# Decay attention and two feed-forward layers on one core: in the first group of each layer every pair of feature tiles takes plain products, and the fourth input sum is made later

## The chip, the core and the metric

The kernel runs as one program on one core of a Trainium2 chip. The time is device time in microseconds (us) of that core, from launch to the last output. Five engines work side by side, each through its own list of instructions in the order in which the program put them there: TensorE (PE) multiplies, with weight loads (PEld) that overlap it; VectorE (DVE), ScalarE (ACT) and GpSimd (POOL) work on tiles in on-chip memory; SyncE (SP) issues transfers. An instruction waits on semaphores until its operands are made and its buffer is free, and whatever stands behind it on its engine waits too.

## The reference

```python
def _attn_ref(q, k, v, lam):              # 2 batches, 8 heads, 768 tokens, head width 64
    ...
    for b in range(nb):                   # blocks of 64 tokens, a state carried from one to the next
        intra = einsum(einsum(qb, kb) * Dmask, vb)
        inter = einsum(qb * lam_pow, kv_state)
        out[:, :, sl] = intra + inter
        kv_state = lam_block * kv_state + einsum(kb * rev_pow, vb)

def _moe_ref(x, w_in, w_out):             # x: 1536 x 512, w_in: 512 x 2048, w_out: 2048 x 512
    h = x @ w_in
    g = h * np.tanh(softplus(h))
    return g @ w_out

def _moe2_ref(x, w_in, w_out):            # the same shapes
    h = x @ w_in
    g = h * sigmoid(h)
    return g @ w_out
```

The attention's output, 1536 tokens of 512 channels, goes through two feed-forward layers without a residual. All data are float32.

## The kernel before, in words

**Precision.** A float32 operand is cut into a high part, rounded by a cast to the matmul's format, and a low part, the difference. A product of two operands is three matmuls: high by high, low by high, high by low. ACT makes the high part (a cast), POOL or DVE the low part (a subtraction). Weights arrive as raw words and DVE first makes a value of them in five instructions (`split_op`, L122 to L138, tile `dec`); in the second layer ACT does the first of the five (L94). Then ACT casts (`wh`) and POOL subtracts (`wl`, `run_parts`, L173).

**Tiles.** Tokens stand in three blocks of 512 (block 0, 1, 2). The 2048 hidden features of a layer are 16 tiles of 128; four tiles are a group, so there are eight groups, g = 0 to 3 in the first layer and 4 to 7 in the second. Two neighbouring tiles are a pair, two pairs to a group. Tile n has an input weight (n,0) and an output weight (n,1).

**Products.** An input product (`emit_h`, L407: 12 matmuls of 128x512 into a bank `ph`) gives one tile of hidden features for one block. `activate` then puts three things behind it: the activation on ACT (`wa`), the cast `gh` on ACT, the low part `gl` on POOL. An output product (`emit_o`, L425: 12 matmuls into four banks `po`) adds that tile to the block's output. After the last tile of a group, `evac` (L457) adds the four banks to `acc` on DVE (in a layer's first group ACT copies them). At the end of the first layer ACT casts `acc` to the next layer's input `xh` and POOL makes `xl`, four of each per block (L474 to L481); the list `rest` holds POOL's part and is drained one entry per item by `run_rest`.

**Block products.** For a pair of feature tiles and token blocks 0 and 1, `Block` (L528) replaces the four input products by seven half-size ones, `m1` to `m7`, of six matmuls each. They need sums of parts of the input (tiles `sh`, `sl`, four sums, made once per layer by `make_sums` in the first and in `evac` in the second) and sums of the pair's weights (`sum_pair`, L145: four subtractions on DVE, tiles `th`, `tl`). Between the seven, ACT copies two intermediate results (`b`, L568; `m5`, L573) and DVE adds two (`c` and `e`, L557). The fourth input sum takes the place of a part of block 1's input (`sums[3]` is `x1[0][:, 0:2]`, L513), so it may be written only after the last plain product of block 1 in that group. Pairs in `plain` (L82) go without block products: pairs 2 and 8, the first pair of groups 1 and 4.

**Order.** The program is written as a list of items per group (L678 to L728). Each item runs its functions and then a few instructions from other lists: `run_parts` (casts and low parts of weights that are ready), `run_rest`, `run_sums` (one entry of the list of input sums) and `run_split(k)` (k instructions of the list of weight splits). Output products of block 2 of a group run as `fills` among the next group's items. Groups 1 and 4 (`first`) begin with four plain input products of pair A, with fills between them, then a block product of pair B among output products, then the output products of block 1 and the input products of block 2 in turn. The other groups have a block product for each pair.

Of the kernel before, what the change touches and what calls it, by code (L numbers as in the profile page):

```python
# [7 lines left out]
F32 = mybir.dt.float32  # L8
# [9 lines left out]
def decay_attention_mish_silu_kernel(  # L18
# [8 lines left out]
    nc = tc.nc  # L27
    P = 128
# [50 lines left out]
    parts = []  # L79

    pre = []
    plain = (2, NF // 2)  # L82
    silu = []
    uses = {}

# [371 lines left out]
    def evac(mm, g, t):  # L457
# [13 lines left out]

        xh, xl = x_tile(t)

        def part(j):  # L474
            nc.scalar.copy(xh[:, j, :], acc[:, j, :])
            rest.append((
                (t, j),
                lambda: nc.gpsimd.tensor_tensor(  # L478
                    out=xl[:, j, :], in0=acc[:, j, :], in1=xh[:, j, :].bitcast(F32), op=ALU.subtract
                ),  # L480
            ))  # L481

        if t != 1:
            for j in range(4):
                part(j)
            return
        a1, a2 = accs[0, 0], acc

# [2 lines left out]
        add, sub = ALU.add, ALU.subtract  # L491
        drain = lambda: run_rest(len(rest))
        summing.extend([
            [tt(f1, a2[:, 0:2], a2[:, 2:4], add)],
            [cast(0, f1), lambda: part(0), lambda: part(1)],
            [low(0, f1), lambda: part(2), lambda: part(3), tt(f1, f1, a1[:, 0:2], sub)],
            [drain, cast(1, f1), tt(f4, f4, f1, sub)],
            [low(1, f1), tt(f3, a1[:, 0:2], f3, sub)],
            [cast(2, f3)],
            [low(2, f3)],  # L500
# [7 lines left out]
    def make_sums():  # L508

        x0, x1 = x_tile(0), x_tile(1)  # L510
        sh, sl = [late[0].tile([P, 3, 2, T], F32R, tag=t, name=t, bufs=1) for t in ("sh", "sl")]
        sums.extend((sh[:, i], sl[:, i]) for i in range(3))
        sums.append((x1[0][:, 0:2], x1[1][:, 0:2]))  # L513
        q = lambda xt, k: [xt[i][:, 2 * k : 2 * k + 2].bitcast(F32) for i in (0, 1)]
        a11, a12, a21, a22 = q(x0, 0), q(x0, 1), q(x1, 0), q(x1, 1)
        tmp = late[1].tile([P, 4, T], F32, tag="acc", name="tmp")
        f1, f2 = tmp[:, 0:2], tmp[:, 2:4]
        f3 = late[0].tile([P, 2, T], F32, tag="t4", name="s3", bufs=1)
        add, sub = ALU.add, ALU.subtract
        summing.extend([  # L520
            [tt(f1, a21[0], a22[0], add), tt(f1, f1, a21[1], add), tt(f1, f1, a22[1], add), tt(f2, f1, a11[0], sub)],
            [cast(0, f1), tt(f2, f2, a11[1], sub), tt(f3, a11[0], a21[0], sub), tt(f3, f3, a11[1], add), low(0, f1)],
            [cast(1, f2), tt(f1, a12[0], f2, sub), tt(f1, f1, a12[1], add), tt(f3, f3, a21[1], sub), low(1, f2)],
            [cast(2, f3), low(2, f3)],
        ])
        last_sum.append([cast(3, f1), low(3, f1)])

    class Block:  # L528

# [105 lines left out]
    for i, (t, f) in enumerate(steps):  # L635
# [6 lines left out]
            make_sums()  # L642
        if i == len(steps) - 1:
            split_pair(3)
            sum_pair(3)
        for half in halves.get(i, ()):
            split_w(*half)
        if n < N:
# [29 lines left out]
    for g in range(1, 2 * NG):  # L678
# [1 line left out]
        pa = n0 // 2  # L680
        A, B = Block(pa), Block(pa + 1)
        o = lambda t, f, a=False, b=False: lambda: emit_o(t, n0 + f, a, b)

        os = [(0, 0), (0, 1), (0, 2), (0, 3), (1, 1), (1, 0), (1, 3), (1, 2)]
        if g == 1:
            os = os[4:] + os[:4]
        os = [o(t, f, i % 4 == 0, i % 4 == 3) for i, (t, f) in enumerate(os)]
        hs = [lambda n=n0 + f: emit_h(2, n) for f in range(GF)]
        sp = lambda fn, *a: lambda: fn(*a)
        more = pa + 2 < NF  # L690
        nxt = [[lambda p=p: split_pair(p)] if p < NF else [] for p in (pa + 2, pa + 3)]
        if nxt[0]:
            nxt[0].append(lambda: sum_pair(pa + 2))
        fill = [[fn, sp(split_w, n0 + j, 1)] for j, fn in enumerate(fills + [idle] * (4 - len(fills)))]
        first = g in (1, NG)
        if g > 1:
            fill[0].append(lambda: sum_pair(pa + 1))
        fill[3] += nxt[0]
        if first:

            order = ((1, 1), (1, 0), (0, 0), (0, 1)) if g == 1 else ((0, 0), (0, 1), (1, 1), (1, 0))
            ha = [[lambda t=t, n=n0 + f: emit_h(t, n)] for t, f in order]
            ha[1 if g == 1 else 3].append(lambda: summing.append(last_sum.pop()))
            items = [it for i in range(4) for it in (ha[i], fill[i])]
        else:
            items = [[A.m1], [A.m5], fill[0], [A.m2], [A.m6], fill[1], [A.m7], [A.m3], fill[2], [A.m4], fill[3]]
        items += [
            [B.m1], [B.m5], [B.m2], [B.m6], [os[0]], [B.m7], [B.m3], [os[1]], [B.m4], [os[2]], [os[3]],
            [hs[0]], [os[4]], [hs[1], *nxt[1]], [os[5]], [hs[2]], [os[6]], [hs[3]], [os[7]],
        ]  # L710
        for at, item in enumerate(items):
            if g == NG and at == 7:
                silu.append(True)
# [2 lines left out]
            for fn in item:  # L716
                fn()
            run_parts(k)
            run_rest(0 if g == NG and 7 <= at < 14 else 1)
            run_sums(1)  # L720
            small = isinstance(getattr(item[0], "__self__", None), Block)
            k = 1 if small else 0 if item[0] is idle else 3 if item[0] in hs or at < (18 if first else 11) else 2
            if g == NG and at < 8:
                k = (0, 1, 1, 1, 1, 3, 3, 3)[at]
            elif g == NG - 1 and at == len(items) - 1:
                k = 0
            run_split(k)
# [51 lines left out]
```

## Time and profile before

| | |
|---|---|
| median of three runs | 606.63 us (605.3 to 607.45) |
| the profiled execution | 607.67 us, its span 605.9 us |
| PE busy | 575.0 us, 95% of the span, 2870 matmuls |
| DVE / ACT / POOL busy | 418.2 / 239.2 / 325.5 us |
| TensorE's granted clock | 0.979 of full speed on average |
| transfers | 50.55 MB, 83 GB/s over the span |

The page's first part is the busy time of each engine, its second cuts the span into 40 slices of 15 us: a digit is the busy share of a slice in tenths, and the PEclk line is the clock that TensorE was granted. Since PE is busy nearly all the time, what is worth reading is where it isn't: a stretch of PE's timeline where starts lie farther apart than elsewhere, the wait printed in brackets, and what the engine named there was itself waiting for.

### The profile page before, as it was taken

The numbers are of one execution on the slowest core, as the hardware profiler recorded it, in microseconds if no ns is written. First come the engines' busy times: TensorE is split into PE (matmuls) and PEld (weight loads), VectorE is DVE, ScalarE is ACT, GpSimd is POOL, SyncE is SP. The second block draws the span as 40 slices with busy tenths as digits, with TensorE's granted clock in tenths as the row PEclk, the third lists the DMA queues.
The fourth block names the chain that finished last, engine by engine and source line by source line (L and its number), as shares of the span: only waits on it lengthen the run. The fifth ranks groups of instructions, "written<-read, shape, count | busy, mean of one in ns | idle before, by whom it ended". The sixth has DMA issues, their size and how long they took to land. (4 is left out here: it accounts for less than half of the span.)

```text
span 605.9 us, 7515 instructions
## 1 busy us (share of the span) xinstructions
PE 575.0 (95%) x2870; PEld 469.3 (77%) x2870; DVE 418.2 (69%) x520; ACT 239.2 (39%) x439; POOL 325.5 (54%) x237
## 2 busy tenths in 40 slices
PE   7899999997899999999999859999999999999997
PEld 4777778886678888888887647788788878888886
DVE  3898963799858687768797779838834895567102
ACT  2435442436413334324426244446433542353220
POOL 1758783346446365646494548737554646445320
PEclk8999999999989999999999879999999999999999
DMA  7955720012322122312221112222402131200103
GB/s 253 421 179 165 288 70 1 1 35 70 104 67 73 36 69 76 98 36 70 70 70 36 35 35 70 69 70 70 133 6 70 46 102 62 70 1 1 70 0 138
DMA packets 14627, 50.55 MB, mean 83 GB/s; under 512 B 1528, under 2 KB 3072, under 8 KB 13312
## 3 DMA queue, kind: packets, MB, share of 16 engines
q1 hardware_dynamic: 14592, 50.08, 24.3%
q8 instruction: 22, 0.36, 0.2%
q14 instruction: 13, 0.11, 0.1%
HBM read 46.92 MB, written 3.15 MB: 83 GB/s over the span
## 5 line engine op out<-in xcount | busy, mean ns | idle before, releaser
L403 POOL TENSOR_TENSOR gl<-wa,gh 128x512 fp32r<-128x512 f32 x96 | 143.8, 1504 | 130.6 <-ACT gh L402 49.1
L179 POOL TENSOR_TENSOR wl<-dec,wh 128x512 fp32r<-128x512 f32 x64 | 88.4, 1381 | 84.9 <-ACT wh L178 84.8
L465 DVE TENSOR_TENSOR acc<-po,acc 128x512 f32<-128x512 f32 x72 | 46.4, 685 | 73.8 <-PE po L441 73.8
L399 ACT ACTIVATE wa<-ph 128x512 f32<-128x512 f32 x48 | 28.8, 599 | 154.2 <-PE ph L418 138.6
L441 PE MATMUL po<-gh,wh 128*128 128x512 f32 x192 | 76.8, 400 | 1.3 <-ACT wh L178 1.3
L418 PE MATMUL ph<-xl,wh 128*128 128x512 f32 x192 | 73.8, 392 | 4.0 <-POOL xl L478 4.0
L441 PE MATMUL po<-gh,wl 128*128 128x512 f32 x192 | 76.1, 396 | 0.9 <-POOL wl L179 0.9
L138 DVE SCALAR_TENSOR_TENSOR dec<-slot,dec 128x512 uint32<-128x512 uint32 x64 | 74.8, 1168 | 1.9
L418 PE MATMUL ph<-xh,wh 128*128 128x512 f32 x192 | 75.7, 394 | 0.2 <-ACT xh L359 0.2
L441 PE MATMUL po<-wl,gh 128*128 128x512 f32 x192 | 74.8, 390 | 0.9 <-POOL wl L179 0.9
L441 PE MATMUL po<-wh,gl 128*128 128x512 f32 x192 | 74.7, 389 | 0.0
L441 PE MATMUL po<-wh,gh 128*128 128x512 f32 x192 | 74.7, 389 | 0.0
L132 DVE TENSOR_SCALAR dec<-dec 128x512 f32<-128x512 f32 x64 | 47.4, 740 | 34.7 <-ACT dec L94 33.6
L136 DVE SCALAR_TENSOR_TENSOR dec<-slot,dec 128x512 uint32<-128x512 uint32 x64 | 60.6, 947 | 2.1
L402 ACT CAST gh<-wa 128x512 fp32r<-128x512 f32 x96 | 58.4, 623 | 1.1
L178 ACT CAST wh<-dec 128x512 fp32r<-128x512 f32 x64 | 39.6, 619 | 44.7 <-DVE dec L138 44.7
L418 PE MATMUL ph<-xh,wl 128*128 128x512 f32 x192 | 53.5, 393 | 0.0
L441 PE MATMUL po<-gl,wh 128*128 128x512 f32 x192 | 51.9, 392 | 0.0
L134 DVE TENSOR_SCALAR dec<-dec 128x512 uint32<-128x512 uint32 x64 | 49.7, 777 | 2.0
L179 POOL TENSOR_TENSOR tl<-t,th 128x512 fp32r<-128x512 f32 x24 | 33.6, 1408 | 24.6 <-ACT th L178 21.0
L418 PEld LDWEIGHTS ph<-xl,wh 128*128 128x128 f32 x192 | 36.0, 188 | 13.0 <-POOL xl L478 5.7
L441 PEld LDWEIGHTS po<-gh,wh 128*128 128x128 f32 x192 | 36.7, 191 | 10.3 <-ACT wh L178 1.7
(106 smaller groups left out, 962.2 us busy)
## 6 DMA issues: line engine op xcount, KB each, us to landing
slot<-w SPq DMA_DIRECT2D x64, 512.0 KB, 3.7
xslot<-x SPq DMA_DIRECT2D x10, 1024.0 KB, 9.0
out<-acc SPq DMA_DIRECT2D x12, 256.0 KB, 2.1
xslot<-x SPq DMA_DIRECT2D x4, 512.0 KB, 4.4
dmask<-scr SPq DMA_DIRECT2D x2, 256.0 KB, 4.5
lamrow<-scr SPq DMA_DIRECT2D x2, 128.0 KB, 6.7
pw<-lam SPq DMA_DIRECT2D x1, 0.0 KB
scr<-pw SPq DMA_DIRECT2D x1, 8.0 KB
```

Of the source, the lines that this page charges most:

```text
L132: nc.vector.tensor_scalar(out=df, in0=df, scalar1=2.0**-15, scalar2=None, op0=ALU.max)
L134: nc.vector.tensor_scalar(out=d, in0=d, scalar1=3, scalar2=0x3FFFFFF8, op0=shl, op1=band)
L136: nc.vector.scalar_tensor_tensor(out=d, in0=low, scalar=29, in1=d, op0=shr, op1=bor)
L138: nc.vector.scalar_tensor_tensor(out=d, in0=high, scalar=0xC0000000, in1=d, op0=band, op1=bor)
L178: nc.scalar.copy(hi, f)
L179: nc.gpsimd.tensor_tensor(out=lo, in0=f, in1=hi.bitcast(F32), op=ALU.subtract)
L399: nc.scalar.activation(a, ps, AF.Mish if mm == 0 else AF.Silu)
L402: nc.scalar.copy(gh, a)
L403: nc.gpsimd.tensor_tensor(out=gl, in0=a, in1=gh.bitcast(F32), op=ALU.subtract)
L418: nc.tensor.matmul(ph, lhsT=wi[wsel][:, kk * P : (kk + 1) * P], rhs=xt[xsel][:, kk, :], start=(i == 0), stop=(i == 3 * KD - 1),)
L441: nc.tensor.matmul(po[t][j], lhsT=lhsT, rhs=rhs, start=(first and wsel + gsel == 0), stop=(last and gsel == 1))
L465: nc.vector.tensor_tensor(out=acc[:, j, :], in0=po[t][j], in1=acc[:, j, :], op=ALU.add)
```

## The change

Pairs 3 and 9 become plain as well, so groups 1 and 4 have no block products at all, and blocks remain in five groups. Those two groups now run: eight plain input products of blocks 0 and 1 (the first four with the fills between them, the last four in turn with the four output products of block 0), then the input products of block 2 in turn with the output products of block 1. The fourth input sum of the first layer is no longer made with the other three but by `fourth`, after the last plain product of block 1, from the second sum's high and low parts in a tile of its own. In the second layer the casts to `xh` of block 1 stand in `evac` itself, ahead of the sums, and POOL's subtractions are drained at the second entry of the list of sums instead of the fourth. The weight sums of pairs 3 and 9 go; those of pairs 4 and 10 are asked for later in the group.

```diff
-    plain = (2, NF // 2)
+    plain = (2, 3, NF // 2, NF // 2 + 1)
...
-        def part(j):
+        for j in range(4):
             nc.scalar.copy(xh[:, j, :], acc[:, j, :])
             rest.append((
...
         if t != 1:
-            for j in range(4):
-                part(j)
             return
...
         summing.extend([
+            [], [drain],
             [tt(f1, a2[:, 0:2], a2[:, 2:4], add)],
-            [cast(0, f1), lambda: part(0), lambda: part(1)],
-            [low(0, f1), lambda: part(2), lambda: part(3), tt(f1, f1, a1[:, 0:2], sub)],
-            [drain, cast(1, f1), tt(f4, f4, f1, sub)],
+            [cast(0, f1)],
+            [low(0, f1), tt(f1, f1, a1[:, 0:2], sub)],
+            [cast(1, f1), tt(f4, f4, f1, sub)],
...
-            [cast(1, f2), tt(f1, a12[0], f2, sub), tt(f1, f1, a12[1], add), tt(f3, f3, a21[1], sub), low(1, f2)],
+            [cast(1, f2), tt(f3, f3, a21[1], sub), low(1, f2)],
...
-        last_sum.append([cast(3, f1), low(3, f1)])
+        def fourth():
+            f4 = late[0].tile([P, 2, T], F32, tag="t4", name="s4", bufs=1)
+            h2, l2 = (s.bitcast(F32) for s in sums[1])
+            for fn in (tt(f4, a12[0], h2, sub), tt(f4, f4, a12[1], add), tt(f4, f4, l2, sub)):
+                fn()
+            summing.append([cast(3, f4), low(3, f4)])
+        last_sum.append([fourth])
...
-            sum_pair(3)
...
-        if nxt[0]:
+        if nxt[0] and not first:
             nxt[0].append(lambda: sum_pair(pa + 2))
...
         if first:
-            order = ((1, 1), (1, 0), (0, 0), (0, 1)) if g == 1 else ((0, 0), (0, 1), (1, 1), (1, 0))
-            ha = [[lambda t=t, n=n0 + f: emit_h(t, n)] for t, f in order]
-            ha[1 if g == 1 else 3].append(lambda: summing.append(last_sum.pop()))
-            items = [it for i in range(4) for it in (ha[i], fill[i])]
+            hp = [[lambda t=t, n=n0 + f: emit_h(t, n)] for t in range(2) for f in range(GF)]
+            hp[-1].append(lambda: summing.append(last_sum.pop()))
+            items = [it for i in range(4) for it in (hp[i], fill[i])]
+            items += [it for i in range(4) for it in (hp[4 + i], [os[i]])]
+            items.append([hs[0], lambda: sum_pair(pa + 2)])
...
-            run_rest(0 if g == NG and 7 <= at < 14 else 1)
+            run_rest(0 if g == NG and 7 <= at < 12 else 1)
...
-                k = (0, 1, 1, 1, 1, 3, 3, 3)[at]
+                k = (1, 1, 1, 2, 2, 2, 2, 2)[at]
```

Three places in the engines' lists follow, each before and after. Numbers behind names tell buffers apart and differ between the two programs.

ACT early in group 1, before. The high part of the weight (4,1) (`wh1_1284`) stands ahead of an activation, its cast, and the copy `b` of the block product.

```order
L399 ACTIVATE wa_1358<-ph_1343 128x512
L402 CAST gh_1356<-wa_1358 128x512
L178 CAST wh1_1284<-dec_1286 128x512
L399 ACTIVATE wa_1386<-ph_1371 128x512
L402 CAST gh_1384<-wa_1386 128x512
L568 COPY b_1406<-a_1399 128x512
L573 COPY m5_1417<-e_1410 128x512
```

ACT at the same place after (`wh1_1278`, `wh1_1325` and `wh1_1358` are the high parts of (4,1), (5,1) and (6,1)).

```order
L399 ACTIVATE wa_1346<-ph_1331 128x512
L178 CAST wh1_1278<-dec_1280 128x512
L402 CAST gh_1344<-wa_1346 128x512
L178 CAST wh1_1325<-dec_1327 128x512
L399 ACTIVATE wa_1376<-ph_1361 128x512
L402 CAST gh_1374<-wa_1376 128x512
L399 ACTIVATE wa_1407<-ph_1392 128x512
L402 CAST gh_1405<-wa_1407 128x512
L178 CAST wh1_1358<-dec_1360 128x512
```

The copies `b` and `m5` are gone; the casts of weights stand among activations of plain products.

ACT in group 4, before: the casts of block 2's input (`xh_802`) and what stands behind them.

```order
L402 CAST gh_2893<-wa_2895 128x512
L475 CAST xh_802<-acc_1328 128x512 x4
L178 CAST th_2903<-t4_2876 128x512
L94 ACTIVATE dec_2940<-slot3_87 128x512
L94 ACTIVATE dec_2944<-slot1_85 128x512
L568 COPY b_2953<-a_2946 128x512
L573 COPY m5_2964<-e_2957 128x512
L178 CAST wh1_2836<-dec_2838 128x512
```

ACT at the same place after; `wh1_2823` is the high part of (17,1), and `ph_2931` is the first input product of block 1.

```order
L402 CAST gh_2884<-wa_2886 128x512
L475 CAST xh_802<-acc_1319 128x512 x4
L178 CAST wh1_2823<-dec_2825 128x512
L94 ACTIVATE dec_2921<-slot3_87 128x512
L94 ACTIVATE dec_2925<-slot1_85 128x512
L94 ACTIVATE dec_2929<-slot0_84 128x512
L399 ACTIVATE wa_2946<-ph_2931 128x512
L402 CAST gh_2944<-wa_2946 128x512
```

What stood behind the four casts was a copy on which the next matmuls wrote; it is now a weight's cast and an activation.

POOL in group 4, before: the four low parts of block 2's input (`xl_803`).

```order
L179 TENSOR_TENSOR wl1_2837<-dec_2838,wh1_2836 128x512
L403 TENSOR_TENSOR gl_2980<-wa_2981,gh_2979 128x512
L179 TENSOR_TENSOR wl1_2909<-dec_2910,wh1_2908 128x512
L478 TENSOR_TENSOR xl_803<-acc_1328,xh_802 128x512
L403 TENSOR_TENSOR gl_3032<-wa_3033,gh_3031 128x512
L403 TENSOR_TENSOR gl_3036<-wa_3037,gh_3035 128x512
```

POOL at the same place after, from the low part of (17,1) to the last of the four.

```order
L179 TENSOR_TENSOR wl1_2824<-dec_2825,wh1_2823 128x512
L403 TENSOR_TENSOR gl_2945<-wa_2946,gh_2944 128x512
L179 TENSOR_TENSOR wl1_2869<-dec_2870,wh1_2868 128x512
L403 TENSOR_TENSOR gl_2985<-wa_2986,gh_2984 128x512
L179 TENSOR_TENSOR wl1_2920<-dec_2921,wh1_2919 128x512
L478 TENSOR_TENSOR xl_803<-acc_1319,xh_802 128x512
L403 TENSOR_TENSOR gl_3023<-wa_3024,gh_3022 128x512
L478 TENSOR_TENSOR xl_803<-acc_1319,xh_802 128x512
L179 TENSOR_TENSOR wl0_2924<-dec_2925,wh0_2923 128x512
L478 TENSOR_TENSOR xl_803<-acc_1319,xh_802 128x512
L403 TENSOR_TENSOR gl_3063<-wa_3064,gh_3062 128x512
L478 TENSOR_TENSOR xl_803<-acc_1319,xh_802 128x512
```

The first of block 2's low parts follows the low part of (19,1), where it followed that of (18,1), and a `gl` or a weight's low part stands between each two of the four.

## Rows read from the trace of the kernel before

**Rows 1.** The page's parts 1 and 2: busy time by engine, and TensorE's granted clock by slice.
```profile
PE 575.0 (95%) x2870; PEld 469.3 (77%) x2870; DVE 418.2 (69%) x520; ACT 239.2 (39%) x439; POOL 325.5 (54%) x237
...
PEclk8999999999989999999999879999999999999999
```

**Rows 2.** Stretches of the span: from:to, length, busy us (instructions), PEclk, DMA.
```profile
144.08:171.31 27.23, 21.74 (x79) 16.76 (x78) 20.34 (x25) 9.94 (x18) 16.80 (x13) 0.87 0.30 97
171.31:320.92 149.61, 149.61 (x662) 123.87 (x660) 113.20 (x148) 54.13 (x95) 83.82 (x59) 1.00 0.21 66
320.92:382.71 61.79, 49.94 (x199) 39.01 (x198) 50.30 (x48) 27.23 (x45) 38.32 (x25) 0.92 0.15 47
382.71:605.90 223.19, 218.46 (x961) 179.75 (x959) 126.04 (x162) 87.74 (x157) 105.10 (x76) 1.00 0.18 59
```

**Rows 3.** Timeline of PE, first stretch: start, us, line, tiles, count, [idle, releaser].
```profile
146.34 0.61 PE L549 MATMUL e<-sl,th 128*128 128x512 f32 x2
150.30 1.07 PE L549 MATMUL a<-xh,wh 128*128 128x512 f32 x2 [3.35 <-ACT b L568]
...
165.71 0.50 PE L441 MATMUL po<-gh,wh 128*128 128x512 f32 x1 [1.25 <-ACT wh L178]
```

**Rows 4.** Timeline of ACT in the first stretch.
```profile
148.00 0.62 ACT L178 CAST wh<-dec 128x512 fp32r<-128x512 f32 x1 [3.44 <-DVE dec L138]
...
149.67 0.58 ACT L568 COPY b<-a 128x512 f32<-128x512 f32 x1
```

**Rows 5.** Timeline of DVE around the first stretch.
```profile
128.51 1.52 DVE L130 TENSOR_SCALAR dec<-slot 128x512 uint32<-128x512 uint32 x1
130.06 0.43 DVE L132 TENSOR_SCALAR dec<-dec 128x512 f32<-128x512 f32 x1
...
137.17 0.43 DVE L164 TENSOR_TENSOR t<-dec 128x256 f32<-128x256 f32 x1
...
142.26 0.41 DVE L130 TENSOR_SCALAR dec<-slot 128x512 uint32<-128x512 uint32 x1
...
146.31 1.66 DVE L138 SCALAR_TENSOR_TENSOR dec<-slot,dec 128x512 uint32<-128x512 uint32 x1
...
162.37 1.40 DVE L132 TENSOR_SCALAR dec<-dec 128x512 f32<-128x512 f32 x1
```

**Rows 6.** Timeline of PE, second stretch.
```profile
337.69 0.50 PE L418 MATMUL ph<-xl,wh 128*128 128x512 f32 x1 [1.47 <-POOL xl L478]
...
358.69 1.22 PE L549 MATMUL a<-xh,wh 128*128 128x512 f32 x2 [7.03 <-ACT b L568]
```

**Rows 7.** Timeline of ACT in the second stretch.
```profile
354.10 2.41 ACT L475 CAST xh<-acc 128x512 fp32r<-128x512 f32 x4 [4.44 <-DVE acc L465]
...
358.06 0.57 ACT L568 COPY b<-a 128x512 f32<-128x512 f32 x1
```

**Rows 8.** Groups by line and shape: busy us, mean ns, idle before, releaser.
```profile
L403 POOL TENSOR_TENSOR gl<-wa,gh 128x512 fp32r<-128x512 f32 x96 | 143.8, 1504 | 130.6 <-ACT gh L402 49.1 <-PE b L549 41.1 <-issue 30.6
L179 POOL TENSOR_TENSOR wl<-dec,wh 128x512 fp32r<-128x512 f32 x64 | 88.4, 1381 | 84.9 <-ACT wh L178 84.8
...
L478 POOL TENSOR_TENSOR xl<-acc,xh 128x512 fp32r<-128x512 f32 x12 | 20.1, 1689 | 0.0
```

**Rows 9.** Timeline of DVE in the second stretch.
```profile
304.31 1.52 DVE L130 TENSOR_SCALAR dec<-slot 128x512 uint32<-128x512 uint32 x1
...
312.01 1.51 DVE L130 TENSOR_SCALAR dec<-slot 128x512 uint32<-128x512 uint32 x1
...
320.44 2.48 DVE L465 TENSOR_TENSOR acc<-po,acc 128x512 f32<-128x512 f32 x4 [1.63 <-PE po L441]
...
336.43 2.28 DVE L455 TENSOR_TENSOR acc<-acc 128x1024 f32<-128x1024 f32 x1
...
353.38 2.47 DVE L465 TENSOR_TENSOR acc<-po,acc 128x512 f32<-128x512 f32 x4
```

**Rows 10.** Timeline of POOL in the second stretch.
```profile
368.83 1.47 POOL L478 TENSOR_TENSOR xl<-acc,xh 128x512 fp32r<-128x512 f32 x1
```

More of the change, by code (lines that the diff above doesn't have):

```diff
@@ L477, in part @@
                 (t, j),
-                lambda: nc.gpsimd.tensor_tensor(
+                lambda j=j: nc.gpsimd.tensor_tensor(
                     out=xl[:, j, :], in0=acc[:, j, :], in1=xh[:, j, :].bitcast(F32), op=ALU.subtract
@@ L682, in decay_attention_mish_silu_kernel @@
         o = lambda t, f, a=False, b=False: lambda: emit_o(t, n0 + f, a, b)
-        os = [(0, 0), (0, 1), (0, 2), (0, 3), (1, 1), (1, 0), (1, 3), (1, 2)]
-        if g == 1:
-            os = os[4:] + os[:4]
+        first = g in (1, NG)
+        os = [(0, 0), (0, 1), (0, 2), (0, 3)] + [(1, f) for f in (range(4) if first else (1, 0, 3, 2))]
         os = [o(t, f, i % 4 == 0, i % 4 == 3) for i, (t, f) in enumerate(os)]
@@ L691, in decay_attention_mish_silu_kernel @@
         nxt = [[lambda p=p: split_pair(p)] if p < NF else [] for p in (pa + 2, pa + 3)]
-        if nxt[0]:
+        if nxt[0] and not first:
             nxt[0].append(lambda: sum_pair(pa + 2))
         fill = [[fn, sp(split_w, n0 + j, 1)] for j, fn in enumerate(fills + [idle] * (4 - len(fills)))]
-        first = g in (1, NG)
-        if g > 1:
+        if not first:
             fill[0].append(lambda: sum_pair(pa + 1))
@@ L699, in decay_attention_mish_silu_kernel @@
         if first:
-            order = ((1, 1), (1, 0), (0, 0), (0, 1)) if g == 1 else ((0, 0), (0, 1), (1, 1), (1, 0))
-            ha = [[lambda t=t, n=n0 + f: emit_h(t, n)] for t, f in order]
-            ha[1 if g == 1 else 3].append(lambda: summing.append(last_sum.pop()))
-            items = [it for i in range(4) for it in (ha[i], fill[i])]
+            hp = [[lambda t=t, n=n0 + f: emit_h(t, n)] for t in range(2) for f in range(GF)]
[3 more added lines that the diff above has]
+            items.append([hs[0], lambda: sum_pair(pa + 2)])
         else:
             items = [[A.m1], [A.m5], fill[0], [A.m2], [A.m6], fill[1], [A.m7], [A.m3], fill[2], [A.m4], fill[3]]
[L707 to L710, printed above, removed]
+            items += [
+                [B.m1], [B.m5], [B.m2], [B.m6], [os[0]], [B.m7], [B.m3], [os[1]], [B.m4], [os[2]], [os[3]], [hs[0]],
+            ]
+        items += [[os[4]], [hs[1], *nxt[1]], [os[5]], [hs[2]], [os[6]], [hs[3]], [os[7]]]
         for at, item in enumerate(items):
@@ L718, in decay_attention_mish_silu_kernel @@
             run_parts(k)
-            run_rest(0 if g == NG and 7 <= at < 14 else 1)
+            run_rest(0 if g == NG and 7 <= at < 12 else 1)
             run_sums(1)
             small = isinstance(getattr(item[0], "__self__", None), Block)
-            k = 1 if small else 0 if item[0] is idle else 3 if item[0] in hs or at < (18 if first else 11) else 2
+            k = 1 if small else 0 if item[0] is idle else 3 if item[0] in hs or at < (8 if first else 11) else 2
             if g == NG and at < 8:
-                k = (0, 1, 1, 1, 1, 3, 3, 3)[at]
+                k = (1, 1, 1, 2, 2, 2, 2, 2)[at]
             elif g == NG - 1 and at == len(items) - 1:
```

## The prediction

> **What bounds the kernel now.** I read the page's first part, then the granted clock by slice, then a table of stretches, then the timelines of PE, ACT and DVE around the two places where PE loses time. PE is busy 95% of the span [rows 1], so the kernel is bound by the number of matmuls, apart from what PE loses in few places. The clock line shows where: it leaves 9 at the very start, in slices 12 and 23 to 24 [rows 1]. The table of stretches gives the loss. From 171.31 to 320.92 us, 660 weight loads (each belongs to one matmul) take 149.61 us: 0.2267 us a matmul, and PE is never idle. At that step the 78 matmuls from 144.08 to 171.31 would take 17.68 us and take 27.23: 9.55 us lost. The 198 from 320.92 to 382.71 would take 44.89 and take 61.79: 16.90 us lost. The 959 after 382.71 would take 217.4 of 223.19 us, and most of the rest is the end of the program [rows 2]. The first stretch is the middle of group 1, the second the first half of group 4: the two groups that the change rewrites. Together they lose 26.45 us.
>
> **Why PE waits there.** In the first stretch the block product `m2` waits 3.35 us for ACT's copy `b` [rows 3]. That copy did not wait for data: on ACT it stood behind the cast of the weight (4,1), which waited 3.44 us for DVE and began at 148.00 us [rows 4], the moment when DVE's last instruction on that weight ended (146.31 + 1.66) [rows 5]. A late weight stops a product that doesn't need it, since the cast is ahead in ACT's list. Later an output product waits for its own weight's cast, 1.25 us [rows 3]. The matmuls behind such a wait run slowly: two take 1.07 us where two took 0.61 before it [rows 3], and the granted clock of the stretch is 0.87 [rows 2], between the levels 2.4 and 1.2 GHz. In the second stretch an input product of block 1 waits for POOL's `xl`, up to 1.47 us each time, and then `m2` waits 7.03 us for `b` [rows 6], which on ACT stood behind four casts of block 2's input that waited 4.44 us for DVE to add up block 2's output [rows 7].
>
> **The change, part by part.** The sum is made against the profiled execution, 607.67 us (span 605.9), which is 1.04 above the median of the runs shown, 606.63.
>
> *More matmuls.* A plain pair is 2 tiles x 2 blocks x 12 = 48 matmuls, a block product 7 x 6 = 42. Two pairs: 12 more, 12 x 0.2267 = +2.72 us, all on the path, since PE is it.
>
> *Work that goes from other engines.* Eight weight subtractions and four adds (DVE), four casts and four copies (ACT), four low parts (POOL); one 1024-wide instruction more for the fourth sum (DVE). Off PE they are worth nothing by themselves; their place in the lists counts below. SP issues the same loads in the same order.
>
> *First stretch: its 9.55 us go.* Up to 144.08 us both programs run the same count of products. From there the new one runs an input product of block 1, then the output products with (4,1), (5,1), (6,1), (7,1) at 146.80, 152.24, 157.68 and 163.12 us (a product is 12 x 0.2267 = 2.72). What is late next, the weights? DVE began (6,0) at 128.51 and ended (7,0) at 137.17, and (4,1) took from 142.26 to 147.97 [rows 5]: (8.66 + 5.71) / 3 = 4.79 us a weight. From 137.17 to 142.26, 5.09 us, it made the weight sums of pair 3 and the fourth sum's low part [rows 5], which no longer stand there. So (4,1) to (7,1) end at 141.96, 146.75, 151.54, 156.33; a cast (0.62, [rows 4]) and a low part (1.38, [rows 8]) later they are 2.8 to 4.8 us ahead of PE. The fourth sum now stands ahead of the addition of block 0's output, whose banks the product at 168.56 needs: (8,0) ends at 161.1, three 1024-wide instructions at up to 2.28 [rows 9] at 168.0, two short ones follow, and the first addition ends about 170. That costs 0 to 2 us; I take 0, since the 2.28 was beside POOL. The copies `b` that PE waited for don't exist any more; the group's activations have four banks and don't hold PE.
>
> *Second stretch: its 16.90 us go, and a new wait of 6.3 comes.* Block 1's `xl` was the first wait; its casts now follow DVE's additions of 320.44 to 322.92 [rows 9] at once, and POOL's four (1.69 each, [rows 8]) end near 330, while the first input product of block 1 comes after eight products, at 320.92 + 8 x 2.72 = 342.7. The copy `b` is gone. Late next is block 2's `xl`. Its input product is the seventeenth: 320.92 + 16 x 2.72 = 364.4, and takes the last quarter of `xl` with its eighth matmul, at 366.0. Block 2's output is ready on PE at 342.7. DVE's list ahead of its additions has six 1024-wide instructions and two weights; the later ones wait for casts behind the activation of the third product (ends 334.5; activation and cast, 336.2), then two sum pieces of up to 2.28 [rows 9] and a weight of 4.79: additions from about 345.3 to 347.8. Before, POOL's first `xl` of block 2 (368.83, [rows 10]) came 13.0 us after the end of these additions (353.38 + 2.47, [rows 9]); between them lay two weights' splits, as now. So 347.8 + 13.0 = 360.8. From there POOL's list has four `xl`, two `gl` and one `wl`: 4 x 1.69 + 2 x 1.50 + 1.38 = 11.1 [rows 8], and the last is ready at 371.9, 5.9 after 366.0. One of the four took only 1.47 [rows 10], so I take 5.3, and 1.0 for the five or so matmuls behind it at the lower clock (0.23 us more each, [rows 3]): 6.3. Bounds: nothing, if POOL starts by 354.9 (additions right after PE, at 342.7 to 345.2, and faster splits). At the other end the additions end as long after PE's end as before: PE ended block 2 at 358.69 - 7.03 less twelve matmuls, 348.9 [rows 6], DVE at 355.85, 6.9 later; now 349.6, POOL starts at 362.6, the last `xl` is ready at 373.7, and with 1.3 for the clock that is 9.0. If the two splits also take 7.70 each instead of 4.79, the slowest in the trace (304.31 to 312.01, [rows 9]), it is 14.8.
>
> *Groups 2, 3 and 5 to 7.* Their lists are the same, and between 171.31 and 320.92 PE loses nothing although DVE is busy 113.2 of 149.6 us [rows 2]; nothing is counted. The cover is DVE's quarter of idle time: gone only if group 1 leaves DVE over 5 us behind.
>
> Sum: 607.67 + 2.72 - 9.55 - 16.90 + 6.3 = 590.2; against the median 1.04 less, **589.2 us**. With the bounds of the second stretch alone 583.9 to 598.7, and 2 us more with the fourth sum late; less 1.0 on the median.
>
> **The rivals.**
>
> *Clean second stretch:* block 2's `xl` is in time. For it: DVE loses two adds, four weight subtractions and its wait for the block product there. Against: POOL's seven instructions take 11.1 us however early they stand. 607.67 + 2.72 - 26.45 = 583.9, 582.9 on the median.
>
> *The second stretch keeps much of its loss:* the chain DVE's additions, four casts, weights, POOL's `xl` was the cause, not the block product, and what PE gains at `b` it waits at `xl`. For it: ACT still has the four casts ahead of a weight's cast and activations, as the order rows show. Against: PE's first use of that weight has until 350.8. Time: 598.7 by the bound above, up to 600.8 with nothing gained there (607.67 + 2.72 - 9.55).
>
> *Slower than before: DVE's splits become the bound.* Both stretches now ask for four output weights earlier, one each 5.44 us, with POOL's `gl` denser beside them. An L132 took 0.43 us at 130.06 and 1.40 at 162.37, under POOL's work [rows 5]. The slowest weight above, 7.70 us, lay in such a place [rows 9]. With w us a weight from 128.51, (7,1) ends at 128.51 + 6w and is wanted at 161.1: it costs from w = 5.43 on. In the second stretch four weights stand ahead of block 2's `xl`: 4 (w - 4.79) on top of 6.3. Both: 10w - 45.5. At 7.70 that is 31.5, and 607.67 + 2.72 - 26.45 + 31.5 = 615.4; slower than before from w = 7.1. Against: 4.79 is the mean of three weights in this very place, with POOL at work.
> The Trainium skill's page "SBUF — State Buffer", section "Who interferes with whom", speaks for this rival: GpSimd and VectorE share a port pair as an exclusive lock, and a VectorE instruction with two inputs in SBUF, or in a two-port mode, waits until GpSimd's instruction has ended. By that rule each of POOL's instructions would hold up one of the split's five for its whole length, and the price would be the 615.4 above if they met every time; the 7.70 agrees with it, the 4.79 shows that they often don't meet.
>
> **Chances.** Forecast (residual wait 2 to 10 us: 585 to 593 on the median) 0.52; clean second stretch 0.16; much of it kept (593 to 600) 0.24; slower 0.05; about as before, by a smaller measure of the same, 0.03. The range reaches from the clean case into the kept one, 582.5 to 598, and leaves out its upper end and the last two. A difference under 0.3% (1.8 us) can't be told from none here. Faster 0.92, same 0.03, slower 0.05.
>
> **What would show it.** Right: from 127.76 us to the end of group 1 PE without a wait and at full clock; no copies `b` before group 2; PE's only waits of note in an input product of block 2 in group 4, on `xl`, in all 3 to 8 us; 2882 matmuls. Wrong: PE waits for a `wh` or `wl` in groups 1 or 4 (the splits), for an addition at the change from block 0's to block 1's output (the fourth sum), or a wait in group 2 that wasn't there. The forecast falls if the sum of PE's waits in group 4 is under 2 or over 10 us.

## The result, and the profile after

The changed kernel takes 591.11 us (median of 4 runs, 589.82 to 591.84), the kernel before 607.04 beside it: ratio 0.9736, 95% interval 0.9703 to 0.9769. The forecast was 589.2. Two kernels of the experiments (e5, e9) had a disturbed execution just where their profile was taken, so each was profiled again (e5b, e9b); all comparisons use undisturbed runs.

From the page of the changed kernel, busy time by engine and TensorE's granted clock, beside [rows 1]:

```profile
PE 572.6 (97%) x2882; PEld 469.1 (80%) x2882; DVE 409.4 (69%) x509; ACT 235.2 (40%) x431; POOL 317.3 (54%) x233
...
PEclk9989999999999999999999998999999999999999
```

There are the 12 more matmuls. The dip of the clock in slice 12 is gone, and of the one in slices 23 to 24 a single slice is left, now the 25th. The table of stretches (columns as in [rows 2]) says the same in time:

```profile
144.08:171.31 27.23, 27.23 (x120) 21.79 (x118) 26.68 (x27) 10.50 (x18) 16.77 (x12) 1.00 0.28 92
171.31:313.76 142.45, 142.45 (x629) 117.98 (x629) 111.64 (x142) 53.02 (x93) 82.99 (x58) 1.00 0.21 68
313.76:359.06 45.30, 45.30 (x200) 37.16 (x198) 38.53 (x40) 23.46 (x37) 29.20 (x21) 1.00 0.21 68
359.06:368.00 8.94, 5.01 (x14) 3.67 (x15) 6.61 (x8) 4.07 (x8) 5.44 (x4) 0.81 0.17 59
368.00:589.00 221.00, 216.97 (x955) 178.65 (x953) 118.03 (x156) 85.51 (x154) 103.11 (x75) 1.00 0.17 58
```

In the 27.23 us that held 78 weight loads there are now 118, and DVE works 26.68 of them. From 127.76 us, where the prediction's list of signs begins, to 359.06 PE has no idle time and the granted clock is 1.00. Nearly all that is left lies within nine microseconds, in PE's timeline there, which answers to [rows 6]:

```profile
358.67 0.39 PE L418 MATMUL ph<-xh,wh 128*128 128x512 f32 x1
360.64 0.50 PE L418 MATMUL ph<-xl,wh 128*128 128x512 f32 x1 [1.58 <-POOL xl L478]
...
363.72 0.51 PE L418 MATMUL ph<-xl,wh 128*128 128x512 f32 x1 [2.35 <-POOL xl L478]
364.06 1.83 PE L418 MATMUL ph<-xh,wl 128*128 128x512 f32 x4
...
368.17 0.39 PE L441 MATMUL po<-wl,gh 128*128 128x512 f32 x1
...
371.13 1.07 PE L418 MATMUL ph<-xh,wl 128*128 128x512 f32 x4
```

This is the input product of block 2, waiting 3.93 us for the last two of its four `xl`; the four matmuls behind take 1.83 us, where four at full clock take 1.07 (at 371.13). From 358.67 to 368.17 PE makes 15 steps in 9.50 us, where 15 x 0.2265 would be 3.40: 6.1 us lost. POOL's timeline (answering to [rows 10]) has the first and the last of the four, and DVE's (to [rows 5, 9]) the output weights, the fourth sum and the additions:

```profile
352.69 1.75 POOL L478 TENSOR_TENSOR xl<-acc,xh 128x512 fp32r<-128x512 f32 x1
...
361.96 1.71 POOL L478 TENSOR_TENSOR xl<-acc,xh 128x512 fp32r<-128x512 f32 x1
```

```profile
129.01 1.52 DVE L130 TENSOR_SCALAR dec<-slot 128x512 uint32<-128x512 uint32 x1
...
137.55 0.42 DVE L130 TENSOR_SCALAR dec<-slot 128x512 uint32<-128x512 uint32 x1
...
156.84 0.69 DVE L138 SCALAR_TENSOR_TENSOR dec<-slot,dec 128x512 uint32<-128x512 uint32 x1
160.17 2.34 DVE L455 TENSOR_TENSOR s<-xh,sh 128x1024 f32<-128x1024 f32 x1
...
168.80 2.47 DVE L465 TENSOR_TENSOR acc<-po,acc 128x512 f32<-128x512 f32 x4
...
313.76 2.48 DVE L465 TENSOR_TENSOR acc<-po,acc 128x512 f32<-128x512 f32 x4 [1.64 <-PE po L441]
...
337.46 2.48 DVE L465 TENSOR_TENSOR acc<-po,acc 128x512 f32<-128x512 f32 x4
```

PE's product on the banks that DVE's additions at 168.80 free, the first of block 1's output:

```profile
169.56 0.47 PE L441 MATMUL po<-gh,wh 128*128 128x512 f32 x1
...
170.12 0.50 PE L441 MATMUL po<-gh,wh 128*128 128x512 f32 x1
...
170.72 0.50 PE L441 MATMUL po<-gh,wh 128*128 128x512 f32 x1
...
171.32 0.50 PE L441 MATMUL po<-gh,wh 128*128 128x512 f32 x1
...
171.89 1.07 PE L441 MATMUL po<-gl,wh 128*128 128x512 f32 x4
```

The four additions take 0.62 us each and end at 169.42, 170.04, 170.65 and 171.27. PE is on time for the first bank and begins each of the other three just behind an addition: the eight steps take 2.33 us, where 8 x 0.2265 would be 1.81. That is 0.5 us lost, though no wait is printed. In e1, e3, e9b and e10 the same eight steps take 2.32 to 2.33 us.

**Three marks** split every execution. A is ACT's activation in the last step of attention, the same in all kernels (125.30 us before, 126.30 after). B is the start of DVE's additions for block 1 at the end of layer 1, which wait for PE (320.44, [rows 9]; 313.76). The third is the end of the span. From the profiles:

| kernel | A | A to B | B to block 2's additions | B to the end |
|---|---|---|---|---|
| before | 125.30 | 195.14 | 32.94 | 285.46 |
| changed | 126.30 | 187.46 | 23.70 | 275.94 |
| e1 layer 1 only | 125.81 | 187.47 | 33.64 | 285.52 |
| e2 layer 2 only | 124.97 | 195.18 | 23.70 | 276.15 |
| e3 `xl` without hold | 125.04 | 187.51 | 23.69 | 271.55 |
| e4 before, ACT's order | 124.34 | 196.81 | 32.94 | 283.75 |
| e5b plain, old DVE load | 125.67 | 193.65 | 23.70 | 274.98 |
| e6 block, no sums | 126.36 | 188.38 | 33.45 | 285.36 |
| e7 heavier splits | 124.78 | 193.94 | 23.70 | 276.78 |
| e8 before, casts at once | 126.01 | 193.42 | 23.90 | 276.17 |
| e9b plain, old casts | 124.98 | 187.47 | 27.91 | 279.75 |
| e10 block, mended | 125.48 | 187.48 | 23.90 | 275.94 |

The change took 7.68 us from layer 1 and 9.52 from layer 2. The attention part took 1.00 more in this execution. Each row of the table is one execution; those of e4 and e9b were 1.9 and 2.6 us faster than the medians of their kernels, 608.62 and 596.6.

### The profile page after: what moved, and what is told of

Same layout as the page of the kernel before. It is cut to its first block, busy times and chain, and to the rows that moved or that the text cites. A ratio compares the mean times of both kernels' runs of the same rounds, so it can differ in the third digit from the quotient of the medians.

```text
span 589.7 us, 7516 instructions
## 1 busy us (share of the span) xinstructions
PE 572.6 (97%) x2882; PEld 469.1 (80%) x2882; DVE 409.4 (69%) x509; ACT 235.2 (40%) x431; POOL 317.3 (54%) x233
## 4 chain that ended last, share of the span: by engine, by line
PE 87%; DVE 6%; DMA 2%; ACT 2%; POOL 1%; issue 1%; SPq 0%; ACTq 0%; POOLq 0%
PE po L441 42%; PE ph L418 24%; PE b L555 7%; PE a L555 4%; PE px L350 3%; PE c L555 2%; PE e L555 2%; PE px L344 1%; PE s L305 1%; DMA dmask<-scr 1%; DVE sm L307 1%; DVE dec L132 1%; DMA slot<-w 1%; DVE dec L134 1%; DVE dec L136 1%
## 5 line engine op out<-in xcount | busy, mean ns | idle before, releaser
L403 POOL TENSOR_TENSOR gl<-wa,gh 128x512 fp32r<-128x512 f32 x96 | 141.2, 1476 | 117.2 <-PE b L555 40.7
L399 ACT ACTIVATE wa<-ph 128x512 f32<-128x512 f32 x56 | 33.5, 599 | 160.4 <-PE ph L418 148.7
L418 PE MATMUL ph<-xl,wh 128*128 128x512 f32 x224 | 86.0, 390 | 3.9 <-POOL xl L478 3.9
L418 PE MATMUL ph<-xh,wh 128*128 128x512 f32 x224 | 88.1, 393 | 0.0
L132 DVE TENSOR_SCALAR dec<-dec 128x512 f32<-128x512 f32 x64 | 49.5, 774 | 40.8 <-ACT dec L94 39.7
L138 DVE SCALAR_TENSOR_TENSOR dec<-slot,dec 128x512 uint32<-128x512 uint32 x64 | 68.4, 1068 | 1.9
L418 PE MATMUL ph<-xh,wl 128*128 128x512 f32 x224 | 62.1, 393 | 0.0
L136 DVE SCALAR_TENSOR_TENSOR dec<-slot,dec 128x512 uint32<-128x512 uint32 x64 | 59.4, 928 | 2.1
L418 PEld LDWEIGHTS ph<-xl,wh 128*128 128x128 f32 x224 | 42.0, 188 | 13.3 <-POOL xl L478 4.8
L418 PEld LDWEIGHTS ph<-xh,wh 128*128 128x128 f32 x224 | 42.0, 188 | 9.5
L418 PEld LDWEIGHTS ph<-xh,wl 128*128 128x128 f32 x224 | 42.4, 189 | 8.8
```

The source lines that it names most:

```text
L132: nc.vector.tensor_scalar(out=df, in0=df, scalar1=2.0**-15, scalar2=None, op0=ALU.max)
L136: nc.vector.scalar_tensor_tensor(out=d, in0=low, scalar=29, in1=d, op0=shr, op1=bor)
L138: nc.vector.scalar_tensor_tensor(out=d, in0=high, scalar=0xC0000000, in1=d, op0=band, op1=bor)
L403: nc.gpsimd.tensor_tensor(out=gl, in0=a, in1=gh.bitcast(F32), op=ALU.subtract)
L418: nc.tensor.matmul(ph, lhsT=wi[wsel][:, kk * P : (kk + 1) * P], rhs=xt[xsel][:, kk, :], start=(i == 0), stop=(i == 3 * KD - 1),)
```

## The experiments

**e1 and e2, one layer at a time.** e1 puts group 4 back, e2 group 1:

```diff
-    plain = (2, 3, NF // 2, NF // 2 + 1)
+    plain = (2, 3, NF // 2)              # e1; e2: (2, NF // 2, NF // 2 + 1)
-        first = g in (1, NG)
+        first, old = g == 1, g == NG     # e2: g == NG, g == 1
...
```

e1: 

> Group 1 as in the changed kernel (pairs 2 and 3 plain), group 4 as before. Theory (each stretch lost its own waits, independent of the other): the first stretch's 9.55 us go, six more matmuls cost 1.36, so 607 - 8.2 = 598.8 us; from the end of group 1 on PE shows the waits of the kernel before, 7.0 us on the copy b at m2 in group 4 among them. Rival (DVE's splits carry what group 1 leaves undone into the later groups): 601 us or more, with PE waits in groups 2 or 3. A side question: the changed kernel's group 1 began 1.0 us later than before; if the edit in the last step of attention does that, group 1 begins 1.0 us late here too, and not if it is the spread of the attention phase.

e2: 

> Group 4 as in the changed kernel (pairs 8 and 9 plain), group 1 as before. Theory: the second stretch loses its 16.90 us and gets 5.6 on POOL's last xl of block 2 (what the changed kernel showed), six more matmuls cost 1.36: 607 - 9.9 = 597.1 us; the first stretch keeps its 9.5 us. The two gains, 8.2 and 9.9, sum to 18.1, against 16 to 17 measured for both together. Rival (the second stretch's gain depends on group 1 being on time): 600 us or more.

Measured: e1 600.43 us (0.9882, 0.9863 to 0.9900), e2 597.71 (0.9834, 0.9818 to 0.9849). In the table each has one of the two gains whole and nothing of the other, so the layers add up. e1 is 1.6 us above its expectation, but PE has no wait in groups 2 and 3, where its rival put one. e1's A is 0.5 later than before and e3, with the changed code there, 0.3 earlier: the late start was spread.

**e3, the place of `xl`.**

```diff
-            run_rest(0 if g == NG and 7 <= at < 12 else 1)
+            run_rest(1)
```

> The changed kernel with one thing undone: in group 4 the list of GpSimd no longer holds block 2's four xl back for five items, so two of them stand ahead of the weight (17,1)'s low part and the others two places apart. Theory (the residual wait is the place of the xl in POOL's list, since POOL idles 4.0, 2.5, 2.0 and 2.3 us between 333 and 351 us): the casts xh end at 340.6, the four xl end near 352 instead of 363.7, PE's waits of 3.9 us and the slow matmuls behind them go, 5.6 us in all, less up to 1 us if the low part of (17,1), now ready at about 349.9, is late for its product at 349.8: 585.5 to 586.5 us. Rival (POOL's amount of work is the bound, not its order): the wait moves to a weight's wl or to a gl and the time stays within 2 us of the changed kernel's 591.

Measured 585.5 us (0.9644, 0.9629 to 0.9659): the interval lies below that of the change. POOL's first and last `xl`, and PE's two waits in that part:

```profile
341.29 2.91 POOL L478 TENSOR_TENSOR xl<-acc,xh 128x512 fp32r<-128x512 f32 x2
...
349.00 1.47 POOL L478 TENSOR_TENSOR xl<-acc,xh 128x512 fp32r<-128x512 f32 x1
```

```profile
349.09 0.50 PE L441 MATMUL po<-wl,gh 128*128 128x512 f32 x1 [0.32 <-POOL wl L179]
...
360.82 0.50 PE L441 MATMUL po<-wh,gh 128*128 128x512 f32 x1 [0.52 <-ACT acc L463]
```

The `xl` are ready at 350.47, and the price is 0.32 us at one low part. The 0.52 us is a wait for ACT's copies of block 0's banks; in the changed kernel they ran at 359.55 to 361.60, while PE waited for `xl`. POOL had time; its order was the limit.

**e4, only ACT's order, in the kernel before.**

```diff
-            run_parts(k)
+            run_parts(0 if g == 1 and 4 <= at < 9 or g == NG and at in (7, 8)
+                      else None if first and at == 9 else k)
+            # block 2's four casts xh also wait until item 9
```

> The kernel before, with ACT's list alone rewritten: in group 1 the cast of the weight (4,1), and in group 4 the casts of block 2's input and of the pending weights, stand behind the copies b and m instead of ahead of them. All block products stay, 2870 matmuls. Theory (a copy behind a cast behind DVE makes the waits, not the block product): the waits of 3.35 and 7.03 us at m2 go, what comes next is an output product on the low part of (4,1) (0.5 to 1 us) and later weights that are as late as before (1.25 and 0.89); about 3 us gained in the first stretch and 6 in the second: 597 to 599 us. Rival (DVE is late with everything, so that the copy only shows it first): PE waits as long one or two products later, and the time stays within 2 us of 607.

Measured 608.62 us (1.0011, 0.9997 to 1.0025): nothing, and my theory of the waits fell. PE's waits now:

```profile
152.50 0.80 PE L441 MATMUL po<-gh,wh 128*128 128x512 f32 x1 [3.78 <-ACT wh L178]
...
354.73 0.73 PE L549 MATMUL a<-xh,wh 128*128 128x512 f32 x2 [2.40 <-ACT b L568]
...
375.80 0.65 PE L441 MATMUL po<-wl,gh 128*128 128x512 f32 x1 [3.12 <-POOL wl L179]
```

In group 1 the copy no longer waits, and PE waits as long at the next output product. What it waits for is not the cast that was moved back: that one, of (4,1), ran at 147.08, 0.45 us after ACT was free. In the kernel before, group 1's output products begin with block 1's and with the second tile, so the first of them takes (5,1), and the cast of (5,1) waited for DVE:

```profile
151.83 0.62 ACT L178 CAST wh<-dec 128x512 fp32r<-128x512 f32 x1 [4.13 <-DVE dec L138]
```

DVE was late with both weights; the copy only showed it first. In group 4 the copy waits 2.40 us instead of 7.03, and two later weights cost 0.55 and 3.12.

**e5b and e6, DVE's load against the form of the products.** e5 gives the plain group DVE's old load:

```diff
-            split_pair(3)
+            split_pair(3), sum_pair(3)
-        last_sum.append([fourth])
+        last_sum.extend([[fourth], [tt(f2, f1, f1, sub)]])   # the second one in group 1's third item
...
```

e6 keeps the block products and drops that load:

```diff
             split_pair(3)
-            sum_pair(3)
-            x = sums[xq] ...
+            x = sums[min(xq, 2) if p == 3 else xq] ...       # and halves of the weights for th, tl
```

e5: 

> The changed kernel, group 1 still plain, but DVE gets back what stood ahead of the output weights of group 1: the four weight sums of pair 3 (computed, cast and lowered, read by nobody) and one 128x1024 instruction for the fourth sum's low part. DVE's list up to (7,1) is then that of the kernel before without its two adds for block products. Theory 1 (these 5.1 us of DVE ahead of the four output weights made the first stretch's loss): (4,1) ends near 142.5 + 5 = 147.5, its low part near 150 where the product wants it at 147.8, so PE waits about 2 us there and little after: 593 to 594 us. Theory 2 (the block products themselves made it: DVE's adds wait for PE while weights stand behind them, so each waits for the other): no wait over 0.5 us in group 1, 591 to 592 us.

e5b: 

> The kernel with DVE's old load in group 1 once more, for a profile whose clock is undisturbed. Its runs took 596.5 us, 5.4 more than the changed kernel, where theory 1 (the place of 5.1 us of DVE work ahead of the output weights) priced 2 to 3. If theory 1 holds with a larger size, PE waits in group 1 for the low part of (4,1) and again for a later weight or for block 0's additions, which stand behind the fourth sum on DVE, 4 to 6 us in all with the slow clock; if something else costs it, group 1 shows no such waits.

e6: 

> The kernel before with pair 3's seven block products, copies and adds as they were, but its weight sums and the fourth input sum left out (the products read the weights' own halves and another sum instead, so their values are not the reference's). This is the opposite of the run with DVE's old load. Theory 1 (DVE's 5.1 us ahead of the output weights): the first stretch's 9.55 us go but for 0 to 1.5: 598 to 599.5 us. Theory 2 (PE and DVE wait for each other through the copies and adds of the block products): most of it stays, 603 us or more, with PE at m2 still waiting for the copy b or an output product for a late cast.

Measured: e5 596.5 us (0.9819, 0.9806 to 0.9833) and e5b 596.12; e6 601.69 (0.9901, 0.9887 to 0.9914), between its two expectations. In the table, layer 1 loses 6.19 us by the load in the plain form and gains 6.76 without it in the block form (5.6 by the medians, 607.32 and 601.69). So in the block form most of the first stretch was this load: DVE's sums, with the casts on ACT and the low parts on POOL that hang on them. Six fewer matmuls (1.36 us) apart, the block form without the load is still 2.28 above the plain one; its one wait there is the copy `b` again:

```profile
149.95 0.73 PE L550 MATMUL a<-xh,wh 128*128 128x512 f32 x2 [1.93 <-ACT b L569]
```

The plain form also asks for the output weights in another order, (4,1) first where it was (5,1); no run tries that by itself. e5b's waits, and TensorE's clock behind the second:

```profile
148.76 0.50 PE L441 MATMUL po<-gh,wl 128*128 128x512 f32 x1 [0.85 <-POOL wl L179]
...
173.63 0.50 PE L441 MATMUL po<-gh,wh 128*128 128x512 f32 x1 [3.04 <-DVE acc L465]
```

```profile
173.60:176.00 2.40, 2.37 (x7) 1.54 (x8) 2.40 (x4) 0.77 (x2) 1.28 (x1) 0.79 0.00 0
176.00:180.00 4.00, 4.00 (x14) 3.14 (x14) 3.86 (x7) 0.97 (x2) 0.58 (x1) 0.70 0.06 16
```

The larger wait is for block 0's additions, behind the fourth sum on DVE. For e5 I had looked for late weights; the size, 6.2 instead of 2 to 3, comes from here. The kernel before has no fourth sum in that place, so e5b does not size its loss: that the two numbers are near each other is chance, and e6 is the measure. Nor is the load quite the old one: it took 5.91 us (137.03 to 142.94) for 5.09 before.

**e7, the slower rival's price.**

```diff
-            split_op(k, raws[n, i], decs[n, i])
+            [split_op(k, ...) for _ in range(2 if k in (0, 1) and (n, i) in heavy else 1)]
```

> The changed kernel with the first two of DVE's five instructions issued twice for the six weights (6,0), (7,0), (4,1), (5,1), (6,1), (7,1) around group 1 (the second time changes no value). The price of the slower rival of the forecast: a weight costs DVE 4.75 us in the changed kernel (129.01 to 157.5 for six); at 0.42 to 1.5 more for each extra instruction, about 0.9, it would be 6.5, and from 5.43 on PE should wait 6 (w - 5.43) in all, less the 1.0 us by which that execution's group 1 began later: about 5.5 us and its slow clock, 596 to 598 us. If the weights were far ahead of PE (the products of group 1 do not hang on DVE's rate), the time stays within 1 us of 591.

Measured 597.22 us (0.9830, 0.9813 to 0.9848), as expected, but not for the reason. A weight took (161.55 - 127.49) / 6 = 5.68 us, for which the rival's formula gives 6 x 0.25 = 1.5 us; layer 1 lost 6.48. PE's waits:

```profile
157.96 0.50 PE L441 MATMUL po<-gh,wl 128*128 128x512 f32 x1 [0.42 <-POOL wl L179]
...
173.31 0.80 PE L441 MATMUL po<-gh,wh 128*128 128x512 f32 x1 [4.16 <-DVE acc L465]
```

Again the additions are what comes late, not the weights. Two pairs of the doubled instruction, from DVE and POOL:

```profile
129.50 0.89 DVE L132 TENSOR_SCALAR dec<-dec 128x512 f32<-128x512 f32 x2
...
133.14 2.90 DVE L132 TENSOR_SCALAR dec<-dec 128x512 f32<-128x512 f32 x2
```

```profile
133.04 1.30 POOL L179 TENSOR_TENSOR wl<-dec,wh 128x512 fp32r<-128x512 f32 x1 [4.32 <-ACT wh L178]
134.29 1.47 POOL L403 TENSOR_TENSOR gl<-wa,gh 128x512 fp32r<-128x512 f32 x1
```

The same pair takes 0.89 us while POOL waits and 2.90 beside POOL's two instructions of 2.77 in all. The Trainium skill's page "SBUF — State Buffer", section "Who interferes with whom", says that a VectorE instruction in a two-port mode, which a `tensor_scalar` can enter, and a GpSimd instruction keep each other out: the later one waits for the other's whole instruction. The durations agree; which mode L132 ran in, no row shows.

**e8, e9 and e10, which part of the change mends layer 2.** e8 makes one edit in the kernel before, e9 undoes the same edit in the changed one:

```diff
-        def part(j):                  # the casts stood among the pieces of the sums
+        for j in range(4):            # ... and now follow the additions at once
             nc.scalar.copy(xh[:, j, :], acc[:, j, :])
...
+            [], [drain],              # the pieces come two items later, xl ahead of them
             [tt(f1, a2[:, 0:2], a2[:, 2:4], add)],
...
```

e8: 

> The kernel before with one part of the change in group 4: block 1's four casts xh follow its last additions at once and its xl are drained in one place, while all block products stay. Theory (each wait of the second stretch is its own): the waits of 1.40, 0.68 and 1.47 us on xl at 334 to 338 and the slow matmuls behind them go, 4 to 5 us: 602 to 603 us. Rival (what PE gains there it loses at the copy b, since that one hangs on DVE's additions for block 2 and the weight sums, not on PE): the wait of 7.03 grows by about 4 and the time stays within 1.5 us of 607.

e9: 

> The changed kernel with block 1's casts and low parts back in their old places among the pieces of the input sums; both groups stay plain. The casts alone, in the kernel before, took 10 us off. Theory (a loop: PE waits for block 1's xl, so ACT's activations and the sum casts behind them come late, so DVE's pieces and block 2's additions behind those come late; it is broken either by earlier casts or by asking for block 1's input four products later, as the plain order does): 591 to 593 us, the same waits as the changed kernel. Rival (only the casts' place matters): 598 to 601 us, with PE waits on xl at about 342 us or DVE's additions for block 2 near 345 to 350 instead of 337.5.

e9b: 

> The plain kernel with block 1's casts in their old places once more, for an undisturbed profile. It took 596.6 us, 5.5 more than the changed kernel, between the two expectations. If the loop through late casts is what is left, PE waits on block 1's xl near 342 us or on DVE's work behind it, and DVE's additions for block 2 begin some us after 337.5; if the loop is broken and only POOL's list got longer, PE's only waits are those on block 2's xl near 361 us, longer by 4 to 5 us than 3.9.

Measured: e8 597.27 us (0.9833, 0.9818 to 0.9848); e9 596.6 (0.9810, 0.9788 to 0.9832). From B to the end the edit alone gives 9.29 us, the plain form with its order alone 5.71, both 9.52. DVE's timeline in e8 shows block 2's additions ahead of the fourth sum's low part:

```profile
343.33 2.47 DVE L465 TENSOR_TENSOR acc<-po,acc 128x512 f32<-128x512 f32 x4
...
349.59 1.23 DVE L452 TENSOR_TENSOR xl<-acc,xh 128x1024 fp32r<-128x1024 f32 x1 [0.18 <-ACT xh L448]
```

Before, that low part stood ahead of the additions (353.38, [rows 9]) and waited for ACT:

```profile
349.17 2.22 DVE L452 TENSOR_TENSOR xl<-acc,xh 128x1024 fp32r<-128x1024 f32 x1 [4.04 <-ACT xh L448]
```

In e8 PE's waits on block 1's `xl` are gone. Its copy `b` waits still, 4.07 us instead of 7.03:

```profile
348.63 1.22 PE L547 MATMUL a<-xh,wh 128*128 128x512 f32 x2 [4.07 <-ACT b L566]
```

e9b's execution took 594.05 us, where the median of e9 is 596.6, so the 5.71 is likely too large. In e9b both expectations were off: the waits on block 2's `xl` are 0.98 and 2.36 us, and a new one is

```profile
341.19 0.76 PE L441 MATMUL po<-wh,gh 128*128 128x512 f32 x1 [3.61 <-DVE acc L465]
```

with block 2's additions 27.91 us behind B instead of 23.70. e8 does not tell the earlier casts from the later pieces.

e10 mends the block form as far as I could:

```diff
+            run_parts(0 if old and at in (7, 8) else None if old and at == 9 else k)
+            [casts.pop(0)() for _ in casts[:] if at >= 9], run_rest(1)
...
```

> Group 1 plain as in the changed kernel; group 4 keeps its block products for the second pair (2876 matmuls, 6 fewer than the changed kernel) but with block 1's casts at once, the copies b and m ahead of block 2's four casts on ACT, and no hold on block 2's xl. Worked out: group 1 plain alone took 600.4, the casts alone took 10.0 off, which makes 590.4; the wait of about 4 us for the copy b (behind DVE's additions and four casts) goes: 586 to 587. Theory (the plain pair of group 4 gains nothing in itself, the order of the casts and low parts does): 584 to 588 us. Rival (block products in that group make PE, ACT and DVE wait for each other whatever the order): 590 us or more, the wait moving from b to a weight's low part, as it did when only ACT's order was changed.

Measured 590.66 us (0.9721, 0.9705 to 0.9737). The theory failed, by these waits:

```profile
346.38 1.19 PE L557 MATMUL b<-sh,th 128*128 128x512 f32 x2 [2.73 <-DVE c L565]
...
356.85 0.50 PE L441 MATMUL po<-wl,gh 128*128 128x512 f32 x1 [1.78 <-POOL wl L179]
...
361.38 0.51 PE L441 MATMUL po<-wl,gh 128*128 128x512 f32 x1 [1.47 <-POOL wl L179]
```

With both orders mended the plain form (e3, 585.5) is 5 us ahead of the block form, though it has six matmuls more: here PE waits for DVE's add and for low parts that now stand behind block 2's `xl` on POOL. Whether another order would free the block form was not tried.

## Why the prediction was right, and where it was not

- **More matmuls, +2.72.** Right: 2882, and the stretch of 142.45 us has 629 weight loads, 0.2265 us each.
- **First stretch, -9.55 and half of 2.72.** Forecast -8.19, measured -7.68. That DVE's weight sums and low part would leave its list ahead of (4,1) was the right term (e6): the six weights took (157.53 - 129.01) / 6 = 4.75 us each, forecast 4.79. Of the 5.09 us that the prediction called work, 1.18 were a wait of DVE for ACT's cast of the fourth sum (at 138.77 in the trace before). That the copy `b` stood behind a late cast was read rightly, but it was not what cost the time: freed of that cast, PE waited as long one product later (e4).
- **The fourth sum, 0 to 2, taken 0.** Nearly: PE's product begins on time at 169.56, and the additions behind the fourth sum then cost it 0.5 us, as much as the first stretch's gain falls short of the forecast (though A to B of the code before varies by more, 193.42 in e8 against 195.14). There was nothing to spare at this place: more work ahead of it on DVE cost 6.2 us (e5b) and 6.5 (e7). The "over 5 us behind" that the prediction gave DVE as slack was said of the groups behind, and there it held: in e5b and e7 PE has no idle time from 180 us to B.
- **Second stretch, -16.90, +1.36, +6.3.** Forecast -9.24, measured -9.52. The waits of the kernel before are gone and the new one has come, so the sum holds for this change. What does not hold is the reason given for the largest of them: "the copy `b` is gone" put its wait down to the block product. The edit in `evac` alone, with the block product kept, gives 9.29, and its copy waits 4.07 us. On top of that edit the plain form gives almost nothing, since it saves this wait and pays with six matmuls and the wait on block 2's `xl`. The rival that blamed the chain through DVE's additions and ACT's casts had the mechanism, and missed that the change itself shortens the chain: block 2's additions come 23.70 us behind B instead of 32.94.
- **The new wait, 5.3 and 1.0.** Found where forecast: 3.93 us of printed wait and 6.1 lost by PE's starts, against 6.3. B is 6.68 earlier in this execution, so the forecast's additions are at 338.6 and POOL's first `xl` at 354.1; measured 337.46 and 352.69. The 13.0 us between the two were copied from the kernel before and came out as 12.75, because the list still held the `xl` back. e3 shows that the wait was to be had for one line, so the rival of the clean second stretch was one line away, and "POOL's seven instructions take 11.1 us however early they stand" was no ground against it.
- **The splits as bound.** Did not come; e7 shows that its price starts earlier than I put it, at the additions and not at the weights.

The sum: 607.67 - 7.68 - 9.52 + 1.00 = 591.47, for 591.51 profiled; since the three parts make up the span, it only shows that none is left out. Against the forecast for this execution, 590.2, it is 0.5 us more in the first stretch, 0.3 less in the second, and 1.0 of late start.

## What to carry to other kernels

A wait's named releaser is only the first place where a late engine shows: move it alone, and the wait goes on to the next product (e4). Ask which list is behind and by how much, then give that load to the new form and take it from the old (e5, e6), before a gain is credited to the form. And when a new wait is forecast on an engine that has idle time ahead of it, look at the order of its list first.

## What the runs showed of the hardware

Equal waits did not cost equal time. Before and in e8, group 1 runs the same code with nearly the same waits (3.35 and 3.36 us at the copy, then 1.25, 0.89 and 0.90), and e8 has one of 0.86 more; yet A to B is 1.72 us shorter in e8. The rows of 144 to 172 us, before and in e8:

```profile
144.00:172.00 28.00, 22.51 (x84) 17.36 (x82) 20.42 (x25) 10.02 (x18) 16.88 (x13) 0.88 0.29 94
```

```profile
144.00:172.00 28.00, 21.59 (x91) 16.46 (x90) 22.43 (x25) 10.72 (x20) 17.80 (x13) 1.00 0.29 94
```

The granted clock is 0.88 in one and 1.00 in the other. So what a wait costs in clock is known here to about 2 us only, and the start of the same attention code varied by as much (A from 124.34 to 126.36).
